# A linear-attention and top-1 MoE kernel: a hand-ordered pipeline over the batches, the expert blocks in two tables, w1 in two halves, unordered scatters

## The chip, the cores and the metric

The kernel runs on one core of one Trainium2 chip. The metric is the device time of one execution in microseconds (us), and of several executions the median. TensorE is called PE, VectorE DVE, ScalarE ACT, GpSimd POOL and SyncE SP. POOL and SP also hand transfers to DMA queues.

## The reference

Two steps follow each other. The first is linear attention over 8 batches with 8 heads, 576 positions and 64 channels, with relu and a cosine and a sine weight of the position. The second is a top-1 mixture of experts on the 4608 rows of 512 numbers that come out.

```
k_p = concat(relu(k) * cos, relu(k) * sin);  q_p likewise
kv  = einsum('bhsf,bhsd->bhfd', k_p, v);  z = k_p.sum(s)
num = einsum('bhsf,bhfd->bhsd', q_p, kv); den = einsum('bhsf,bhf->bhs', q_p, z) + 1e-6
x = (num / den), rows of 512
logits = x @ w_gate;  expert = argmax;  gate = softmax(logits)[expert]
h = relu(x @ w1[expert]);  out = gate * (h @ w2[expert])   # 8 experts, 512 -> 1024 -> 512
```

An expert takes at most 1152 rows; rows above that give zero.

## The kernel before

**Attention, one batch after the other.** A batch loads k, v and q (1.18 MB each, fp32) over SP's queue: k and v in rows of 1 KB (L173), q in transfers that gather 256-byte pieces (L168). ACT takes the relu of k (L185). DVE multiplies v with the cosine and the sine table in 16 operations of 128x256 and 4 tails of 64x256 (L196, L200). PE makes the kv products (L211), transposes them (L217) and makes the gate columns from them (L223), so that the attention product gives the router's logits too. PE transposes q (L234), and ACT takes the relu while it moves q out of PSUM (L235). Ten units follow: PE forms p (L252) in one of two PSUM buffers, ACT scales half of it (L258), DVE adds the other half and writes `num` (L260).

**Router.** A chain of small DVE operations (L266 to L328) divides, finds each row's expert and, with a few small PE products (L296 to L309) and the running count `carry`, the row's slot. DVE and POOL write the scaled rows in bf16 with the token's number behind them (`xg`, L336), and POOL scatters them in five indirect transfers into the DRAM buffer `xd` (L341), which keeps a region for each expert. Behind each batch's scatters POOL issues one expert's w1 (L347, 2.1 MB read as fp32, 1 MB written as bf16).

**Experts.** After the last batch POOL issues eight pieces of w2 (L353), ACT writes zero rows behind each expert's last row (L360), and DVE makes one table of 43 blocks (L363 to L402): a block is 128 rows of one expert, and the table holds its expert and its first row. `first(i)` fetches a block transposed (`xT`, L420) and its token numbers (`ids`, L422), multiplies with w1 (`h_ps`, L431, 8 matmuls), relu on ACT (L434), and transposes on PE (L437) into `hT` (L439). `second(i)`, 17 blocks behind, multiplies with w2 (`y_ps`, L448), copies on ACT or DVE in turn into one of four `y` buffers (L452, L454) and scatters the rows to `out` (L455).

**What sets the order.** The tile framework's scheduler places each engine's instructions from the program as written, and adds the waits. Both kinds of scatter are declared free of dependences within a group (L344, L458), but no instruction is a member of that group, so that each scatter waits for the landing of the one before; this is seen in the waits below.

Of the kernel before, what the change touches and what calls it, by code (L numbers as in the profile page):

```python
# [26 lines left out]
def kernel(  # L27
# [99 lines left out]
    carry = state.tile([P, E], FP32, name="carry", tag="carry")  # L127
    nc.vector.tensor_copy(out=carry[:], in_=base[:])

    scatters = "xd rows"  # L130

    with ExitStack() as p1:
        pc = p1.enter_context(tc.tile_pool(name="pc", bufs=1))

        vs_t = []
        for i in range(2):
            t_ = pc.tile([P, NC, HB, 2, D + 1], FP32, name=f"vs{i}")
            for c in range(NC):
# [12 lines left out]
        kvp = p1.enter_context(tc.tile_pool(name="kvp", bufs=2))
        kv1 = p1.enter_context(tc.tile_pool(name="kv1", bufs=1))
# [5 lines left out]
        def load(src, b, name):  # L158
# [17 lines left out]
            if name != "q":  # L176
                nc.sync.dma_start(out=t[:], in_=src[b, :, NJ * P:S, :].rearrange("h p d -> p h d"))
# [228 lines left out]
    with ExitStack() as p2:  # L406
# [93 lines left out]
```

## Time and profile of the kernel before

| what | value |
|---|---|
| three executions | 550.68 us median (548.35 to 555.81) |
| profiled execution | 557.07 us, span of its instructions 555.3 us |
| mean granted clock of PE | 0.836 of full speed |
| busy: PE, DVE, ACT, POOL | 357.1, 213.6, 159.3, 133.5 us |
| moved by DMA | 66.98 MB, mean 121 GB/s |
| from the start to batch 1's kv products | 45.35 us |
| batches 1 to 7 | 45.35 to 257.90 us |
| w2 awaited | 257.90 to 317.60 us |
| experts | 317.60 to 555.30 us |

The shares of busy time are means over stages that differ, so the stretches are read apart. The granted clock is a share of full speed: 1.0 is 2.4 GHz and 0.5 is 1.2 GHz. "A <- B" in a list of waits says that A stood idle until B was done. In the chain that ended last, each piece is what released the next; "issue" is time in which nothing that the profile shows was awaited.

### The profile page before, as it was taken

Reading aid. Unit: us, or ns where it says so; the run is one execution under the profiler, and the core shown is the slowest. Engines: PE = TensorE matmul, PEld = TensorE weight load, DVE = VectorE, ACT = ScalarE, POOL = GpSimd, SP = SyncE. Lnnn points to the kernel's source line nnn. Section 1 sums busy time; section 2 is a strip of 40 time slices with the busy share of each in tenths; the row PEclk is TensorE's granted clock in tenths of the full one; section 3 lists DMA queues with packets and bytes.
Section 4 is the critical chain, followed back from the end, with each engine's and each line's share of the span. In section 5 each row is a group of like instructions: output and inputs, shape, how many; then the busy total and the mean of one; then the engine's idle time right before and its main releaser. Section 6 shows DMA issues by size and latency. Waiting matters only on the chain.

```text
span 555.3 us, 8309 instructions
## 1 busy us (share of the span) xinstructions
PE 357.1 (64%) x2672; PEld 222.3 (40%) x2672; DVE 213.6 (38%) x614; ACT 159.3 (29%) x288; POOL 133.5 (24%) x159
## 2 busy tenths in 40 slices
PE   0867675695886767671000187999999988895520
PEld 0645555573764646461000043444444433442210
DVE  1468582665839386738200013222222222210000
ACT  4262604225251525241000042433333323310000
POOL 4003251232423233434340000002222212222222
PEclk9897867669767779797555598999999999999985
DMA  5983879688776753518999931424334231011210
GB/s 152 235 208 105 213 132 263 120 210 173 184 173 124 194 86 111 87 39 156 163 186 223 178 52 30 77 48 86 86 85 111 61 86 57 29 73 54 77 67 30
DMA packets 113449, 66.98 MB, mean 121 GB/s; under 512 B 80151, under 2 KB 105751, under 8 KB 113408
## 3 DMA queue, kind: packets, MB, share of 16 engines
q0 software_dynamic: 17776, 31.37, 26.9%
q1 hardware_dynamic: 94480, 34.02, 26.8%
q10 hardware_dynamic: 1152, 1.05, 0.7%
q8 instruction: 24, 0.39, 0.3%
q14 instruction: 17, 0.14, 0.1%
HBM read 61.92 MB, written 17.06 MB: 142 GB/s over the span
## 4 chain that ended last, share of the span: by engine, by line
PE 38%; DMA 29%; issue 11%; DVE 10%; ACT 7%; SPq 3%; POOL 1%; POOLq 0%; DVEq 0%; ACTq 0%
DMA out_dram<-y,idx 15%; PE kv_ps L211 10%; PE h_ps L431 9%; PE p_ps L252 6%; DMA w_sb<-in_moe_w_dram 5%; PE y_ps L448 5%; DMA km<-in_k_dram 4%; DVE num L260 4%; ACT tmp L258 3%; DMA xd<-xg,slot_i 3%; PE ht_ps L437 2%; PE q_ps L234 2%; PE g_ps L223 1%; ACT km L185 1%; DVE lg L272 1%
## 5 line engine op out<-in xcount | busy, mean ns | idle before, releaser
L431 PE MATMUL h_ps<-w_sb,xT 128*128 x344 | 87.3, 390 | 61.7 <-DMA w_sb<-in_moe_w_dram 60.0
L448 PE MATMUL y_ps<-w_sb,hT 128*128 x344 | 82.5, 378 | 20.6 <-DVE y L454 8.1
L455 POOL DMA_INDIRECT out_dram<-y,idx x43 | 41.8, 972 | 217.1 <-ACT h L434 96.1
L434 ACT ACTIVATE h<-h_ps 128x512 bf16<-128x512 f32 x86 | 51.4, 597 | 143.5 <-PE h_ps L431 143.5
L252 PE MATMUL p_ps<-kva,rq 64*128 64x146 f32 (+1 forms) x640 | 64.9, 338 | 21.4 <-DVE num L260 20.0
L341 POOL DMA_INDIRECT xd<-xg,slot_i x40 | 46.6, 1165 | 123.1 <-DMA xd<-xg,slot_i 75.4
L431 PEld LDWEIGHTS <-xT 128*128 128x128 bf16 x344 | 33.6, 100 | 97.7 <-DMA xT<-xd 58.9
L260 DVE SCALAR_TENSOR_TENSOR num<-p_ps,sintab,tmp 128x292 f32<-128x292 f32 (+1 forms) x80 | 40.9, 519 | 67.1 <-ACT tmp L258 63.4
L252 PEld LDWEIGHTS p_ps<-kva,rq 64*128 64x128 f32 (+1 forms) x640 | 50.7, 206 | 33.4 <-DVE num L260 30.3
L211 PE MATMUL kv_ps<-vs,km 128*64 128x130 f32 x512 | 51.8, 365 | 14.5 <-DVE vs L196 14.5
L448 PEld LDWEIGHTS <-hT 128*128 128x128 bf16 x344 | 32.8, 97 | 56.3 <-issue 26.3
L439 DVE COPY hT<-ht_ps 128x1024 bf16<-128x1024 bf16 x43 | 29.6, 690 | 55.6 <-PE ht_ps L437 52.0
L424 DVE TENSOR_TENSOR idx<-ids,pen 128x1 int32<-128x1 int32 x43 | 6.8, 159 | 114.6 <-DMA ids<-xd 72.0
L258 ACT ACTIVATE tmp<-p_ps,costab 128x292 f32<-128x292 f32 (+1 forms) x80 | 39.9, 503 | 33.4 <-PE p_ps L252 29.2
L211 PEld LDWEIGHTS kv_ps<-vs,km 128*64 128x64 f32 x512 | 40.8, 187 | 21.7 <-issue 21.6
L437 PE MATMUL ht_ps<-identb,h 128*128 128x128 bf16 x344 | 34.4, 223 | 9.6 <-DVE hT L439 5.1
L336 POOL TENSOR_TENSOR xg<-num,rden 128x512 bf16<-128x512 f32 x16 | 23.1, 1464 | 67.0 <-DVE rden L328 58.8
L437 PEld LDWEIGHTS <-h 128*128 128x128 bf16 x344 | 22.8, 99 | 36.0 <-ACT h L434 27.1
L454 DVE COPY y<-y_ps 128x512 f32<-128x512 f32 x22 | 15.2, 692 | 52.0 <-DMA out_dram<-y,idx 37.4
L452 ACT COPY y<-y_ps 128x512 f32<-128x512 f32 x21 | 12.3, 587 | 71.8 <-DMA out_dram<-y,idx 36.2
L336 DVE TENSOR_TENSOR xg<-num,rden 128x512 bf16<-128x512 f32 (+1 forms) x24 | 27.1, 1182 | 0.2
L196 DVE TENSOR_SCALAR vs<-vm,costab 128x256 f32<-128x256 f32 x64 | 22.3, 348 | 11.0 <-DMA vm<-in_v_dram 10.8
(113 smaller groups left out, 296.1 us busy)
## 6 DMA issues: line engine op xcount, KB each, us to landing
w_sb<-in_moe_w_dram POOLq DMA_DIRECT2D x16, 1024.0 KB, 10.1
km<-in_k_dram SPq DMA_DIRECT2D x16, 512.0 KB
vm<-in_v_dram SPq DMA_DIRECT2D x16, 512.0 KB
qm<-in_q_dram SPq DMA_DIRECT2D x64, 128.0 KB
xd<-zrow ACTq DMA_DIRECT2D x8, 128.5 KB
kt<-in_k_dram SPq DMA_DIRECT2D x8, 128.0 KB
vt<-in_v_dram SPq DMA_DIRECT2D x8, 128.0 KB
qt<-in_q_dram SPq DMA_DIRECT2D x32, 32.0 KB
```

The source lines that it names most:

```text
L211: nc.tensor.matmul(out=kv_v[o * D:(o + 1) * D, r, :, :], lhsT=lhsT, rhs=rhs, start=(c == 0), stop=(c == NC - 1))
L252: nc.tensor.matmul(out=p_ps[0:rows, o, r, 0:2 * KW], lhsT=rq[o * D:(o + 1) * D, 2 * u + r, c * P:c * P + rows], rhs=kva[o * D:(o + 1) * D, ...
L258: nc.scalar.activation(out=tmp[0:rows], in_=p_v[0:rows, :, 0:KW], func=ACT.Copy, scale=costab[0:rows, c:c + 1])
L260: nc.vector.scalar_tensor_tensor(out=num[0:rows, c, u * HB:(u + 1) * HB, :], in0=p_v[0:rows, :, KW:2 * KW], scalar=sintab[0:rows, c:c + 1] ...
L336: eng.tensor_tensor(out=xg[0:rows, c, 0:DT].rearrange("p (h d) -> p h d", h=H), in0=num[0:rows, c, :, 0:D], in1=rden[0:rows, c, :].unsquee ...
L341: si = nc.gpsimd.indirect_dma_start(out=xd[:, :], out_offset=bass.IndirectOffsetOnAxis(ap=slot_i[0:rows, c:c + 1], axis=0), in_=xg[0:rows, ...
L431: nc.tensor.matmul(out=h_ps[:], lhsT=xT[:, g, :], rhs=w1_sb[:, bass.ds(e1, 1), g, n * 512:(n + 1) * 512], start=(g == 0), stop=(g == G - 1))
L434: nc.scalar.activation(out=h[:, n * 512:(n + 1) * 512], in_=h_ps[:], func=ACT.Relu)
L437: nc.tensor.transpose(out=t_ps[:, f, :], in_=h[:, f * P:(f + 1) * P], identity=identb[:])
L439: nc.vector.tensor_copy(out=hT[:], in_=t_ps[:])
L448: nc.tensor.matmul(out=y_ps[:], lhsT=hT[:, f, :], rhs=w2_sb[:, bass.ds(e2, 1), f, :], start=(f == 0), stop=(f == FB - 1))
L455: oi = nc.gpsimd.indirect_dma_start(out=out[:, :], out_offset=bass.IndirectOffsetOnAxis(ap=idx[:, 0:1], axis=0), in_=y[:], in_offset=None, ...
```

## The change

All instructions are now placed by the program's own order (`tc.manual_schedule()`). `run()` merges several lists of steps by a fraction between 0 and 1 that each list gets. An iteration `it` of the attention holds three stages: `stage_a(it)` (relu of k, scaling of v, q's transposes, kv products and gate columns), `stage_p(it-1)` (the ten p units) and `stage_r(it-2)` (router and scatters). Loads are issued an iteration ahead. q comes in rows of 1 KB, and its relu goes to POOL (`relu_q`, four operations of 128x512 and two of 64x256 for a batch). v is scaled in eight operations of 128x512 on DVE, its two tails go to ACT, and so do the two copies of the gate columns. `vs` and `qm` have one buffer.

w1 is held in two halves: `w1a`, columns 0 to 511 of each expert, is loaded in iterations 2 to 8; `w1b` takes memory that the attention frees, so that it comes after it. `table_a` is made after seven batches and holds 24 full blocks; `table_b`, after the last batch's router, holds the other 19. The first halves of seven blocks are multiplied with `w1a` among the steps of the last batch's router. Then w1b's eight pieces, w2's eight pieces, the second halves of the seven blocks, and the loop over the rest, with `down(i)` 17 blocks behind as before. Scatters are now members of their groups. `y` has two buffers in place of four, `xT` ten in place of six.

```diff
-    NB = (N + E * (P - 1)) // P
-    LAG = 17
...
+    NA = -(-(N - S - E * (P - 1)) // P)
+    NB = (N + E * (P - 1)) // P - NA
+    HA, HX = 7, 18
+    LAG = 17
+    FIRST = 7
...
+    def free_of(ins, group):
+        tc.declare_no_dep(ins.ins, group=group, reason=DISJOINT)
+
+    def member(ins, group):
+        tc.add_to_no_dep_group(group, ins.ins)
+
+    def run(*streams):
+        order = []
+        for n, (steps, lo, hi) in enumerate(streams):
+            for i, f in enumerate(steps):
+                order.append((lo + (hi - lo) * (i + 0.5) / len(steps), n, i, f))
+        for _, _, _, f in sorted(order, key=lambda t: t[:3]):
+            f()
+
+    ctx.enter_context(tc.manual_schedule())
...
+    yp = ctx.enter_context(tc.tile_pool(name="yp", bufs=2))
...
+        for name, src in (("k", k), ("v", v), ("q", q)):
+            pl = io1 if name == "q" else io
+            m = pl.tile([P, H, NJ, D], FP32, name=name + "m", tag=name + "m")
+            t = pl.tile([D, H, D], FP32, name=name + "t", tag=name + "t")
+            nc.sync.dma_start(out=m[:], in_=src[b, :, 0:NJ * P, :].rearrange("h (p j) d -> p h j d", j=NJ))
+            nc.sync.dma_start(out=t[:], in_=src[b, :, NJ * P:S, :].rearrange("h p d -> p h d"))
+            loaded[b][name] = (m, t)
...
-                            nc.sync.dma_start(out=m[:, r, :, o, :],
-                                              in_=sv[r, 0:NJ * P, o, :].rearrange("(p j) d -> p j d", j=NJ))
...
+        def relu_q(w):
+            def f():
+                u, r = w // 2, w % 2
+                nc.gpsimd.tensor_scalar(
+                    out=qr[:, w, :, :, :].rearrange("p j o d -> p o j d"),
+                    in0=qm[:, u * HB + r:u * HB + r + 3:2, :, :], scalar1=0.0, scalar2=None, op0=ALU.max)
...
+                if c == NJ:
+                    nc.scalar.activation(out=vs[0:rows, c, :, t, 0:D], in_=src, func=ACT.Copy,
+                                         scale=tab[0:rows, c:c + 1])
...
+        steps += [emit(0), emit(1), emit(2), scatter(0), emit(3), scatter(2), emit(4), scatter(1), scatter(4),
+                  scatter(3)]
...
+                free_of(si, "xd rows")
+                if b == B - 1:
+                    free_of(si, "early reads")
+                member(si, "xd rows")
...
+    def w1_piece(n, e):
+        def f():
+            nc.gpsimd.dma_start(out=w1h[n][:, e, :, :],
+                                in_=moe_w1[e].rearrange("(g p) f -> p g f", p=P)[:, :, n * 512:(n + 1) * 512])
...
+    load(0)
+    for it in range(B + 1):
+        streams = []
+        if it < B:
+            load(it + 1)
+            elem, rls, qs, kvst = stage_a(it)
+            streams += [(elem, 0.0, 0.5), (rls, 0.0, 0.3), (qs, 0.1, 0.5), (kvst, 0.45, 1.0)]
+        if 1 <= it:
+            streams.append((stage_p(it - 1), 0.05, 0.97))
+        if 2 <= it:
+            streams.append((stage_r(it - 2, ps_a, "a"), 0.0, 1.0))
+            streams.append(([w1_piece(0, it - 2)] + ([w1_piece(0, 7)] if it == B else []), 0.9, 1.0))
+        run(*streams)
+    table_a()
...
+        ti = nc.sync.dma_start(out=xT[:], in_=xd[bass.ds(r0, P), 0:DT], transpose=True)
+        ids = const.tile([P, 2], BF16, name=f"ids{i}")
+        di = nc.sync.dma_start(out=ids[:], in_=xd[bass.ds(r0, P), DT:XW])
+        if i < NA:
+            member(ti, "early reads")
+            member(di, "early reads")
...
+    def up(i, n):
...
+        h = hp.tile([P, F // 2], BF16, name="h", tag=f"h{n}")
...
+            nc.tensor.matmul(out=h_ps[:], lhsT=bl["xT"][:, g, :], rhs=w1h[n][:, bass.ds(e1, 1), g, :],
...
+        y = yp.tile([P, DT], FP32, name="y", tag="y")
...
+        free_of(oi, "out rows")
+        member(oi, "out rows")
...
+    htx = []
+    firsts = [lambda i=i: fetch(i) for i in range(2)]
+    for i in range(FIRST):
+        firsts.append(lambda i=i: fetch(i + 2))
+        firsts.append(lambda i=i: up(i, 0))
+        if i >= 1:
+            firsts.append(lambda i=i: turn(i - 1, 0))
+    firsts.append(lambda: turn(FIRST - 1, 0))
+    run((firsts, 0.0, 1.0), (stage_r(B - 1, ps_y, "y"), 0.0, 0.6), ([table_b], 0.6, 0.7),
+        ([w1_piece(1, e) for e in range(E)], 0.65, 1.0))
     for e in range(E):
         nc.gpsimd.dma_start(out=w2_sb[:, e, :, :], in_=moe_w2[e].rearrange("(g p) d -> p g d", p=P))
...
-        yp = p2.enter_context(tc.tile_pool(name="yp", bufs=4))
...
-            tc.declare_no_dep(oi.ins, group="out rows", reason=DISJOINT)
...
-        for i in range(NB + LAG):
-            if i < NB:
-                first(i)
-            if i >= LAG:
-                second(i - LAG)
+    nump.release()
+    rt.release()
+    htx.append(ctx.enter_context(tc.tile_pool(name="htx", bufs=HX)))
+    NBLK = NA + NB
+    for i in range(FIRST):
+        up(i, 1)
+        if i >= 1:
+            turn(i - 1, 1)
+    turn(FIRST - 1, 1)
+    for i in range(FIRST, NBLK + LAG):
+        if FIRST + 2 <= i + 2 < NBLK:
+            fetch(i + 2)
+        if i < NBLK:
+            up(i, 0)
+            up(i, 1)
+        if FIRST <= i - 1 < NBLK:
+            turn(i - 1, 0)
+            turn(i - 1, 1)
+        if 0 <= i - LAG:
+            down(i - LAG)
```

**PE in one batch of the attention.** Before, PE's row of a batch from the second half of the kv products on (`kv_ps`, `t_ps` and `g_ps` its transposes and gate columns, `q_ps` and `qt_ps` q's transposes, `p_ps` the p units):

```order
L211 MATMUL kv_ps<-vs_151,km 64x130 x8
L211 MATMUL kv_ps<-vs_151,kt 64x130 x2
L217 MATMUL t_ps<-ident,kvt 128x128 x4
L223 MATMUL g_ps<-wg_sb,t_sb 128x32 x4
L234 MATMUL q_ps<-ident,qm 128x128 x16
L240 MATMUL qt_ps<-ident,qt 128x64 x4
L252 MATMUL p_ps<-kva,rq 128x146 x32
L252 MATMUL p_ps<-kva,rq 64x146 x8
```

After, the end of one iteration and the start of the next on PE (`p_ps` belongs to the batch before that of `kv_ps` and `q_ps`):

```order
L291 MATMUL kv_ps<-vs,km 64x130 x8
L291 MATMUL kv_ps<-vs,kt 64x130 x2
L329 MATMUL p_ps<-kva,rq 64x146 x4
L303 MATMUL t_ps<-ident,kvt 128x128 x4
L329 MATMUL p_ps<-kva,rq 64x146 x4
L312 MATMUL g_ps<-wg_sb,t_sb 128x32 x4
L329 MATMUL p_ps<-kva,rq 128x146 x4
L262 MATMUL q_ps<-ident,qr 128x128 x4
L329 MATMUL p_ps<-kva,rq 128x146 x4
```

The p units no longer stand in one piece behind their own batch's transposes, but one at a time among another batch's kv products and transposes.

**POOL at the last batch and the weights.** Before (`xd` the scatters of the last batch, `w_sb` w2; DMASW is a lane of POOL's transfers, and a wait on it is for a landing):

```order
L341 DMA xd<-xg,slot_i 37888x514 [waits DMASW3_49]
L353 DMA w_sb<-in_moe_w_dram 128x8x512
L341 DMA xd<-xg,slot_i 37888x514 [waits DMASW5_49]
L353 DMA w_sb<-in_moe_w_dram 128x8x512
L341 DMA xd<-xg,slot_i 37888x514 [waits DMASW7_49,DMASW1_49]
```

After, the same place, with the last scatters of the last batch and the first pieces of `w1b`:

```order
L493 DMA xd<-xg,slot_i 37888x514 [waits DMASW6_49,DVE_49]
L493 DMA xd<-xg,slot_i 37888x514 [waits DMASW7_49,Pool_49]
L508 DMA w1b<-in_moe_w_dram 128x4x512 [waits DMAHW3_49,DMAHW2_49,DMAHW4_49,DMASW0_49,DMAHW5_49,PE_49,Activation_49]
L508 DMA w1b<-in_moe_w_dram 128x4x512 [waits DMASW1_49]
L508 DMA w1b<-in_moe_w_dram 128x4x512 [waits DMASW2_49]
```

The weights stood between the scatters; now all of `w1b`, and behind it all of w2, stand behind the last scatter, and the first piece waits for the attention's readers.

**POOL at the end.** Before, the scatters to `out`, each with the lane of the scatter ahead of it:

```order
L455 DMA out_dram<-y,idx 4608x512 [waits DMASW5_49,DMASW4_49,Activation_49]
L455 DMA out_dram<-y,idx 4608x512 [waits DMASW6_49,DMASW5_49,DVE_49]
L455 DMA out_dram<-y,idx 4608x512 [waits DMASW7_49,DMASW6_49,Activation_49]
L455 DMA out_dram<-y,idx 4608x512 [waits DMASW7_49,DVE_49]
L455 DMA out_dram<-y,idx 4608x512 [waits DMASW0_49,Activation_49]
```

After:

```order
L693 DMA out_dram<-y,ix 4608x512 [waits DMASW0_49,DVE_49]
L693 DMA out_dram<-y,ix 4608x512 [waits DMASW1_49,DVE_49,Activation_49]
L693 DMA out_dram<-y,ix 4608x512 [waits DMASW2_49,DVE_49]
L693 DMA out_dram<-y,ix 4608x512 [waits DMASW3_49,DVE_49,Activation_49]
L693 DMA out_dram<-y,ix 4608x512 [waits DMASW4_49,DVE_49]
```

Each now waits for its own lane alone, which is that of the scatter eight before it, and for its `y`.

## Rows read from the trace of the kernel before

**Rows 1.** Stretches: length, busy time (count) of PE, PEld, DVE, ACT, POOL; clock, DMA share, GB/s.

```profile
45.35:257.90 212.55, 151.00 (x1436) 120.63 (x1435) 133.87 (x392) 76.40 (x150) 70.31 (x63) 0.79 0.66 150
257.90:317.60 59.70, 0.01 (x1) 0.11 (x2) 8.57 (x29) 0.00 (x0) 15.68 (x15) 0.50 1.13 189
317.60:369.30 51.70, 44.90 (x275) 22.01 (x275) 13.38 (x35) 20.31 (x34) 0.00 (x0) 0.93 0.34 53
431.00:489.00 58.00, 49.98 (x281) 23.00 (x280) 14.04 (x29) 16.78 (x29) 11.63 (x12) 1.00 0.21 59
489.00:555.30 66.30, 30.03 (x133) 12.65 (x131) 6.23 (x9) 4.69 (x8) 17.44 (x18) 0.86 0.16 60
```

**Rows 2.** The same columns for single batches, from kv products to kv products.

```profile
73.65:108.73 35.08, 24.24 (x207) 19.68 (x209) 19.22 (x58) 11.23 (x22) 11.22 (x11) 0.69 0.75 173
202.93:230.47 27.54, 19.26 (x207) 15.48 (x209) 19.70 (x58) 9.69 (x20) 9.89 (x9) 0.87 0.43 94
```

**Rows 3.** Waits of POOL: us in all, times, longest.

```profile
POOL xd L341 <- DMA xd<-xg,slot_i: 75.4, 19, 7.5
POOL out_dram L455 <- DMA out_dram<-y,idx: 49.6, 18, 5.3
```

**Rows 4.** The chain that ended last, 264 to 318 us: start, length, what.

```profile
264.26 0.94 POOL w_sb L353
...
290.36 27.19 DMA w_sb<-in_moe_w_dram
317.59 3.57 PE h_ps L431 x8
```

**Rows 5.** Timeline of PE, one batch: start, length, engine, line, operation, count, idle before.

```profile
202.86 2.00 PE L211 MATMUL kv_ps<-vs,km 128*64 128x130 f32 x16
...
210.01 1.11 PE L211 MATMUL kv_ps<-vs,km 128*64 128x130 f32 x16
...
211.41 0.98 PE L217 MATMUL t_ps<-ident,kvt 128*128 128x128 f32 x4
213.39 1.08 PE L223 MATMUL g_ps<-wg_sb,t_sb 128*128 128x32 f32 x8 [0.99 <-ACT t_sb L219]
214.30 1.95 PE L234 MATMUL q_ps<-ident,qm 128*128 128x128 f32 x16
...
218.42 1.27 PE L252 MATMUL p_ps<-kva,rq 64*128 64x146 f32 x16 [0.73 <-DVE num L260]
```

**Rows 6.** The chain that ended last, in the p units of an earlier batch.

```profile
158.24 2.50 PE p_ps L252 x16
```

**Rows 7.** Groups by form, DVE, 45 to 258 us: operation, count, busy, mean ns, idle before.

```profile
L260 DVE SCALAR_TENSOR_TENSOR num<-p_ps,sintab,tmp 128x292 f32<-128x292 f32 x56 | 28.6, 521 | 52.9 <-ACT tmp L258 49.2 <-ACT rq L242 2.5 <-issue 1.1
L196 DVE TENSOR_SCALAR vs<-vm,sintab 128x256 f32<-128x256 f32 x48 | 17.1, 357 | 0.0
L200 DVE TENSOR_SCALAR vs<-vt,sintab 64x256 f32<-64x256 f32 x12 | 4.2, 348 | 0.1
```

**Rows 8.** Groups by form, POOL, the whole span.

```profile
L341 POOL DMA_INDIRECT xd<-xg,slot_i x40 | 46.6, 1165 | 123.1 <-DMA xd<-xg,slot_i 75.4 <-issue 18.8 <-DVE num L260 17.5
...
L336 POOL TENSOR_TENSOR xg<-num,rden 128x512 bf16<-128x512 f32 x16 | 23.1, 1464 | 67.0 <-DVE rden L328 58.8 <-DVE last L373 8.1
```

**Rows 9.** The chain that ended last in the steady part of the experts, one block to the next.

```profile
373.46 1.73 PE h_ps L431 x8
...
377.68 1.80 PE h_ps L431 x8
```

**Rows 10.** Timeline at the end: an evict, its scatter and w2's matmuls, and the last scatter.

```profile
516.49 0.69 DVE L454 COPY y<-y_ps 128x512 f32<-128x512 f32 x1 [6.29 <-DMA out_dram<-y,idx]
517.14 0.97 POOL L455 DMA_INDIRECT out_dram<-y,idx  x1 [2.51 <-DMA out_dram<-y,idx]
517.24 1.89 PE L448 MATMUL y_ps<-w_sb,hT 128*128 x8 [1.72 <-DVE y L454]
...
549.17 0.97 POOL L455 DMA_INDIRECT out_dram<-y,idx  x1 [2.41 <-DMA out_dram<-y,idx]
```

More of the change, by code (lines that the diff above doesn't have):

```diff
@@ new lines @@
+    tmpp = pool("tmpp", 2)
+    ps_a = pool("ps_a", 4, bass.MemoryType.PSUM)
+    ps_p = pool("ps_p", 2, bass.MemoryType.PSUM)
+    vs = io1.tile([P, NC, H, 2, D + 1], FP32, name="vs")
+    for c in range(NC):
+        for t, tab in ((0, costab), (1, sintab)):
+            nc.gpsimd.tensor_copy(out=vs[:, c, :, t, D:D + 1],
+                                  in_=tab[:, c:c + 1].unsqueeze(1).to_broadcast([P, H, 1]))
+    num_t = []
+    for i in range(2):
+        t_ = nump.tile([P, NC, H, KW], FP32, name=f"num{i}")
+        nc.gpsimd.memset(t_[D:P, NJ, :, :], 1.0)
+        num_t.append(t_)
@@ L314 @@
[L314 to L317 removed]
+            nc.tensor.matmul(out=st["d"][:, 0, :], lhsT=ub[0:D, :], rhs=oh[0:D, NJ, :], start=False, stop=False)
+            nc.tensor.matmul(out=st["d"][:, 1, :], lhsT=onesb[0:D, :], rhs=oh[0:D, NJ, :], start=False, stop=True)
@@ L338, with scatter, f @@
                     in1=rden[0:rows, c, :].unsqueeze(2).to_broadcast([rows, H, D]), op=ALU.mult)
-            for c in range(NC):
+            return f
+        def scatter(c):
+            def f():
                 rows = P if c < NJ else D
@@ new lines, in table_b @@
+    def table_b():
+        end_i = tp.tile([P, E], I32, name="end_i")
+        nc.vector.tensor_copy(out=end_i[:], in_=carry[0][:])
+        for e in range(E):
+            r0 = nc.values_load(end_i[0:1, e:e + 1], engines=[ACTE], min_val=e * REG, max_val=e * REG + N,
+                                skip_runtime_bounds_check_because=INRANGE)
+            zi = nc.scalar.dma_start(out=xd[bass.ds(r0, P), :], in_=zrow[:])
+            free_of(zi, "xd rows")
+            free_of(zi, "early reads")
+            member(zi, "xd rows")
+        todo = whole("b", True)
+        nc.vector.tensor_tensor(out=todo[:], in0=todo[:], in1=tabs["done"][:], op=ALU.subtract)
+        tbl, _, pn = table("b", NB, todo[:], tabs["done"], True)
+        tabs["b"], tabs["pen"] = tbl, pn
@@ new lines, in up @@
+    def up(i, n):
+        bl = blocks[i]
+        tbl, m = where(i)
+        e1 = nc.values_load(tbl[0:1, 0, m:m + 1], engines=[PE], min_val=0, max_val=E - 1,
+                            skip_runtime_bounds_check_because=INRANGE)
+        h = hp.tile([P, F // 2], BF16, name="h", tag=f"h{n}")
+        h_ps = ps_h.tile([P, 512], FP32, name="h_ps", tag="h")
+        for g in range(G):
+            nc.tensor.matmul(out=h_ps[:], lhsT=bl["xT"][:, g, :], rhs=w1h[n][:, bass.ds(e1, 1), g, :],
+                             start=(g == 0), stop=(g == G - 1))
+        nc.scalar.activation(out=h[:], in_=h_ps[:], func=ACT.Relu)
+        bl["h", n] = h
```

590 lines of the change are left out of this document (332 added, 258 removed).

## The prediction

> **What bounds the kernel now.** I read the stretches first, then the single batches, the waits, the chain that ended last, and last the timelines. Batches 1 to 7 take 212.55 us, 30.4 us each. No engine fills them: PE is busy for 151.00 us, DVE for 133.87, and the DMA share is 0.66 [rows 1]. A batch's own steps stand in a row, so the engines wait for each other: DVE's `num` additions alone were preceded by 49.2 us of waiting for ACT's `tmp` [rows 7]. PE also runs slowly. The granted clock is 0.79 in this stretch, 0.69 in the slowest batch (35.08 us) and 0.87 in a fast one (27.54 us) [rows 1, 2]; sixteen p matmuls take 2.50 us at the low level (1.2 GHz) and 1.27 at the high one (2.4 GHz) [rows 5, 6]. Then come 59.70 us with PE at rest, in which w2 is awaited: its first piece is issued at 264.26 and the first expert matmuls start at 317.59 [rows 1, 4]. The experts follow. While up and down run together a block takes 377.68 − 373.46 = 4.2 us, nearly all PE [rows 9]. From 431 us on PE is the bound no more: scatters wait for scatters, 49.6 us in 18 waits [rows 3], and in the last 66.30 us PE is busy for 30.03 [rows 1].
>
> **The attention.** All of PE's work in an iteration at the high level: kv four times 211.41 − 210.01, 5.6; t 0.98; g 1.08; q's transposes and tail 2.4; five pairs of p units at 1.27, 6.35; the router's products 0.7: 17.1 us [rows 5]. (The last two small numbers are read from the row of q, 1.95, and its tail, and from the gaps of the same batch.) DVE is busy 19.70 us in a batch now [rows 2]. It loses sixteen operations of 0.357 and four of 0.348 (7.1 us) and two small copies (0.4, an estimate), and gains eight operations of 128x512. No row of DVE has that form: below lies 0.357 for half the size, above twice that, 0.71 [rows 7]. I take 0.61, nearer to the upper end because it is twice the work: 4.9. DVE's sum is 17.1. ACT gets v's tails and the gate copies and gives nothing back in number of operations (q's still move out of PSUM on ACT): about 13 from the 9.69 to 11.23 of now [rows 2], no bound. POOL gets the relu of q. The row for a 128x512 operation on POOL is 1.464, with two inputs; below it I only have DVE's 0.357 for half the size. I take 1.0 for each of four and 0.6 for each of two, 5.2 us; with two `xg` (2.9), five scatters (5.8 by their mean of 1.165) and one weight issue (0.94) POOL has 15 us [rows 4, 8]. The scatters no longer wait for each other: 75.4 us of POOL's idle time goes [rows 3], but POOL was not the bound in the attention, and I count nothing for it. It is covered by the two engines at 17.
>
> An iteration isn't as short as its busiest engine, since `vs` has one buffer. In its first half DVE must scale v (4.9), half of the p units (5 times 0.521) and half of the router chain (about 3.2), so 11 us, before the kv products can run; in the second half PE has kv, half of p and the gate columns, 10.6, and the evictions between them, about 2.5 [rows 5, 7]. That gives **24 us an iteration**, against 30.4. The bounds: 20, if the halves overlap so that DVE's 17.1 and some 3 us of waits are left; 31, if PE stays at the low level, where 2.00 stands for 1.11 [rows 5]: 17.1 by 1.8. Iteration 0 waits for all of q before the transposes and has no other batch to work on; I take 40 us (before, batch 1's kv products begin at 45.35, [rows 1], with the router of batch 0 already in it). Iteration 1 lacks the router: 20. Six full ones 144, and iteration 8, without `stage_a`, 14: the last `num` at 218, the table 3.3 behind it, so T0 = 221. Before, that stretch ends at 257.90. **Gain in the attention: 36 us.** q in rows of 1 KB instead of 256 bytes takes load off SP's queue; the DMA share is 0.66 on average, so the loads are hidden by the 24 us of an iteration (and if they weren't, 3.54 MB at the 173 GB/s of a busy batch take 20 us, less than 24) [rows 1, 2].
>
> **The weights.** Half of w1 is now late: w1b (8.4 MB read) is loaded after the attention, with w2 (16.8 MB) behind it in the same queue. What waits: POOL's first w1b issue stands behind the last batch's scatters, and those behind its router, whose PE products stand behind the first `up` of block 0, which waits for batch 6's scatters and the last pieces of w1a. I take 9 us for that, 9 more for the router chain, 3 for `xg` and 5 for the five scatters: first issue at T0 + 26 (20 to 35). The rate: w2's 16.8 MB took 317.59 − 264.26 = 53.3 us, with the DMA share at 1.13 [rows 1, 4]. The 25.2 MB take 80 us by that, and with the blocks' fetches among them I take 91. So the last w2 piece lands at W2 = T0 + 117 = 338, later than the 317.6 of now. This eats most of what the attention gave. By the Trainium skill, page "DMA: Bandwidth & Descriptors", section "Specifications", a core's share of the memory is about 358 GB/s, so that 25.2 MB would take 70 us and the sum would be 10 us lower; the trace's own rate is 315 GB/s, and it is the one that I use.
>
> **The experts.** In the time to W2 PE does up of 17 blocks in two helpings, with pauses of some 26 and 19 us. The downs wait for all of w2. From W2: 1.73 for the first down, 25 pairs at 4.25 [rows 9], 106.3; then 17 downs alone. Now each costs the serial scatter: the evict to `y`, 0.1, the landing, next scatter, 3.4 us a block (66.30 us for the last of them) [rows 1, 10]. Unordered, a block costs the larger of PE's matmuls (1.89 for eight, [rows 10]), POOL's 0.97, and half of a turn of `y`'s two buffers, which is the evict, 0.69, and the landing. From one scatter's start to the next pass 0.97 + 2.51, and the next evict lies in that, so a landing comes about 2.8 after its start [rows 10]: (0.69 + 0.1 + 2.8)/2 = 1.8. I take 1.8, 30.6 us. PE starts after pauses at the low level: 6 us lost, as the clock of 0.93 over 51.70 us cost about 4 now [rows 1]. The last scatter's end: 6.8, from 555.3 − 549.17 = 6.1 and its evict [rows 10]. W2 + 1.7 + 106.3 + 30.6 + 6 + 6.8 = W2 + 151.4 = 489.5 us of span. Now the same part, from 317.59 to 555.3, is 237.7 us, of which 17 ups (about 44 us) move ahead of W2 and the rest is the scatters'.
>
> **Sum.** 489.5 against a span of 555.3; the profiled execution adds 1.8 (557.07), so 491.3. That execution stands 6.4 us above the median of 550.68, and I take it off: **485 us**.
>
> **Rivals.**
> - *The halves overlap and the clock stays high.* Two batches' products in one stream leave PE fewer gaps. T = 20 and no loss by the clock: 6 × 4 + 6 less, about 455 us. For it: DVE's 17.1. Against it: the single `vs`.
> - *PE stays at the low level through the attention.* T = 31, the attention gains nothing: 6 × 7 more, 42 us, and the early up blocks slow as well (about 12): some 540, no change. For it: PE would be busy for 17 of 24 us, a smaller load than the 24.24 of 35.08 us that stands beside clock 0.69 [rows 2]. By the Trainium skill, page "TensorE: Matmul & The Clock Gate", section "HAM oscillation — how this bites in real kernels", idle gaps between groups of matmuls drop the clock again and again; the trace agrees in that the first eight up matmuls after the 59.70 us at rest took 3.57 us, later ones 1.73.
> - *Two `y` buffers bring the tail back.* If a landing takes 6 us with several scatters under way, in place of 2.8, a block costs 3.4 us in the tail: 17 × 1.6 more, about 512 us. For it: POOL's longest wait for a landing was 5.3 us [rows 3]. Against it: it was one of 18 that came to 49.6.
> - *POOL's queue decides, and the kernel gets slower.* The relu of q stands in POOL's order ahead of `xg` and the scatters of another batch, and q's transposes wait for it. If one operation on its strided form takes 4 us instead of 1.0, POOL's sum is 27 and its chain, in which `relu_q` waits for q and `xg` for the router, about 36: 6 × 12 more, then the later w1a and scatters, 571 us. It decides from T = 33 on. Against it: 1.464 for the two-input operation of that size [rows 8].
>
> **How the numbers follow.** Main case 0.55 (its own range 470 to 510: T from 22 to 26, 12 us each way, and 8 us of the weights' 91); the fast attention 0.19; y's buffers 0.10; the low clock 0.10; POOL 0.06. The range 455 to 530 takes in the first three, 0.84, and leaves out no change and slower. About 2% (11 us) can be told from no change: faster 0.84, within 2% 0.10, slower 0.06.
>
> **What would show it.** Right: iterations of 24 us from one batch's kv products to the next; DVE operations on `vs` of 0.6 and `qr` on POOL of 1.0; the first w1b issue near 247 us and the last w2 landing near 338; pairs of 4.25 with no wait for w2 after that; the last 17 downs at 1.8, with no scatter waiting for a scatter. Wrong: clock under 0.7 in the attention; `qr` above 2 us; evicts that wait for scatters in the list of waits; w1b and w2 taking over 100 us, which would put each microsecond on the end.

## The result and the profile after

| | before | after |
|---|---|---|
| median, lowest and highest of four executions | 553.24 us (548.35 to 556.31) | 501.01 us (497.33 to 501.60) |
| profiled execution, its span | 557.07, 555.3 us | 497.33, 495.5 us |
| ratio of the times | | 0.905 (95%: 0.896 to 0.914) |
| mean granted clock of PE | 0.836 | 0.852 |
| busy: PE, DVE, ACT, POOL | 357.1, 213.6, 159.3, 133.5 us | 349.4, 185.3, 170.6, 192.1 us |

The change is faster by 9.5%. Forecast were 485 us and faster; 501 lies in the range of 455 to 530. The steps behind that number came out worse and better than forecast, by amounts that mostly cancel, so they are read one by one. Two profiled executions below are slow ones, those of the run with ordered scatters to `xd` (574.85 us, median 562.3) and of the run with w1b in iteration 8 (498.69 us, median 492.8).

The stretches of the changed kernel, in the columns of [rows 1]: one iteration of the attention, the first 31 us of awaiting weights, the rest of that time, the blocks in which up and down run together, and the end.

```profile
143.21:170.67 27.46, 19.66 (x206) 15.06 (x206) 14.98 (x45) 12.96 (x27) 16.63 (x16) 0.81 0.60 170
275.12:306.37 31.25, 2.90 (x13) 1.48 (x13) 2.23 (x8) 1.20 (x2) 13.02 (x17) 0.50 1.17 190
306.37:356.50 50.13, 37.17 (x225) 19.16 (x224) 10.53 (x27) 17.32 (x29) 0.07 (x1) 0.87 1.28 192
356.50:457.62 101.12, 101.12 (x616) 51.91 (x616) 28.16 (x66) 37.10 (x63) 24.42 (x25) 0.99 0.35 92
457.62:495.50 37.88, 30.48 (x139) 13.19 (x136) 8.88 (x28) 5.07 (x9) 17.50 (x18) 0.96 0.20 77
```

Against [rows 1, 2]: this iteration takes 27.5 us in place of the 27.5 to 35.1 of a batch, at a clock of 0.81 in place of 0.69 to 0.87. From one batch's kv products to the next's, which is called the pitch below, five iterations take 142.5 us (73.88 to 216.41), 28.5 each. The blocks in which up and down run together fill PE wholly (101.12 of 101.12 us), at 3.9 us a block in place of the 4.2 of [rows 9]. The end takes 37.9 us in place of 66.3. The time in which weights are awaited has become longer, 81.4 us from 275.12 to 356.50 in place of 53.3 [rows 4], but PE is busy for 40 of them. The span is 59.8 us shorter: w2 is first used 38.9 us later than the experts began before (356.5 against 317.6), and what follows takes 98.7 us less (139.0 against 237.7), in part because 17 ups now stand ahead of it.

**What closes an iteration.** The timeline of PE in the same iteration (columns as in [rows 5]), then a wait:

```profile
169.29 1.08 PE L312 MATMUL g_ps<-wg_sb,t_sb 128*128 128x32 f32 x8
170.67 1.00 PE L329 MATMUL p_ps<-kva,rq 64*128 64x146 f32 x8 [0.30 <-ACT kva L315]
177.28 1.12 PE L262 MATMUL q_ps<-ident,qr 128*128 128x128 f32 x4 [5.62 <-POOL qr L217]
```

```profile
PE q_ps L262 <- POOL qr L217: 28.1, 5, 5.7
```

That is PE's wait for `qr` from 60 to 230 us (us in all, times, longest). POOL, and DVE in the next iteration:

```profile
165.32 1.55 POOL L485 TENSOR_TENSOR xg<-num,rden 128x512 bf16<-128x512 f32 x1 [9.41 <-DVE rden L478]
167.04 1.10 POOL L493 DMA_INDIRECT xd<-xg,slot_i  x1 [0.17 <-POOL xg L485]
...
174.32 1.03 POOL L493 DMA_INDIRECT xd<-xg,slot_i  x1 [0.30 <-issue]
175.42 0.24 POOL L374 TENSOR_SCALAR xg<-tok_i 128x5 int32<-128x5 int32 x1
175.74 5.84 POOL L217 TENSOR_SCALAR qr<-qm 128x512 f32<-128x512 f32 x4
...
193.67 1.55 POOL L485 TENSOR_TENSOR xg<-num,rden 128x512 bf16<-128x512 f32 x1 [10.30 <-DVE rden L478]
```

```profile
180.32 0.52 DVE L336 SCALAR_TENSOR_TENSOR num<-p_ps,sintab,tmp 128x292 f32<-128x292 f32 x1 [5.14 <-ACT tmp L334]
...
183.68 0.19 DVE L411 TENSOR_TENSOR oh<-key,kmx 128x40 bf16<-128x40 f32 x1
...
193.39 0.19 DVE L478 TENSOR_TENSOR rden<-rden,gate 128x40 f32<-128x40 f32 x1
```

PE has done the gate columns and one p unit by 171.7 and then waits 5.6 us for `qr`. POOL makes `qr` at 175.74, not because q is late, but because `xg` and five scatters stand ahead of it in POOL's order. These wait for `rden`, the end of another batch's router, whose small operations stand in DVE's order between `num` additions that wait, over ACT's `tmp`, for PE: the one at 180.32 waits 5.14 us, as PE had waited for `qr`. So the loop is: `qr`, PE's products, DVE's router, `xg`, scatters, the next `qr`. POOL is busy for 16.6 of 27.5 us and idles for nearly 11 of them, and yet its order sets the pitch; the first experiment below tests this. The sizes of the operations with new forms, by groups:

```profile
L217 POOL TENSOR_SCALAR qr<-qm 128x512 f32<-128x512 f32 x32 | 46.8, 1485 | 30.5 <-DMA qm<-in_q_dram 30.1
L245 DVE TENSOR_SCALAR vs<-vm,costab 128x512 f32<-128x512 f32 x32 | 16.6, 518 | 15.1 <-DMA vm<-in_v_dram 15.1
L245 DVE TENSOR_SCALAR vs<-vm,sintab 128x512 f32<-128x512 f32 x32 | 15.6, 487 | 0.0
```

**Where the weights' time begins.** PE's timeline around the last batch's router, POOL's issues, and PE at the first w2 products:

```profile
259.68 1.87 PE L660 MATMUL h_ps<-w1a,xT 128*128 x4 [18.07 <-DMA xT<-xd]
261.35 0.31 PE L424 MATMUL c_ps<-oh,ub 128*128 128x32 bf16 x4
```

```profile
275.12 6.08 POOL L508 DMA_DIRECT2D w1b<-in_moe_w_dram  x8
...
305.56 0.87 POOL L711 DMA_DIRECT2D w_sb<-in_moe_w_dram  x1 [2.27 <-DMA w1b<-in_moe_w_dram]
```

```profile
356.50 3.34 PE L681 MATMUL y_ps<-w_sb,hT 128*128 x8 [6.48 <-DMA w_sb<-in_moe_w_dram]
```

In PE's order the router's products (`c_ps`) stand behind the first block's `up`, which waits 18 us for its rows. They lead to the last scatters, and these to w1b's first issue at 275.12. From there the 25.2 MB that w1b and w2 read take until 356.5.

### The profile page after: what moved, and what is told of

It is laid out like the page before. It is cut to its first block, busy times and chain, and to the rows that moved or that the text cites. A ratio compares the mean times of both kernels' runs of the same rounds, so it can differ in the third digit from the quotient of the medians.

```text
span 495.5 us, 8167 instructions
## 1 busy us (share of the span) xinstructions
PE 349.4 (71%) x2672; PEld 219.3 (44%) x2672; DVE 185.3 (37%) x544; ACT 170.6 (34%) x319; POOL 192.1 (39%) x205
## 4 chain that ended last, share of the span: by engine, by line
PE 31%; issue 24%; POOL 19%; DMA 15%; SPq 4%; DVE 3%; ACT 2%; another core or an unknown queue 1%; POOLq 1%; ACTq 0%; DVEq 0%
PE h_ps L660 13%; PE y_ps L681 9%; POOL qr L217 7%; POOL xd L493 5%; DMA xT<-xd 5%; DMA out_dram<-y,ix 4%; DMA qm<-in_q_dram 4%; PE ht_ps L671 3%; PE kv_ps L291 2%; POOL xg L485 2%; PE p_ps L329 2%; DMA ids<-xd 2%; POOL qrt L222 2%; POOL out_dram L693 1%
## 5 line engine op out<-in xcount | busy, mean ns | idle before, releaser
L329 PE MATMUL p_ps<-kva,rq 64*128 64x146 f32 (+1 forms) x640 | 77.0, 356 | 3.9 <-ACT kva L315 2.4
L672 DVE COPY hT<-ht_ps 128x512 bf16<-128x512 bf16 x86 | 33.2, 420 | 119.8 <-PE ht_ps L671 107.9
L660 PE MATMUL h_ps<-w1a,xT 128*128 x172 | 47.2, 399 | 43.1 <-DMA xT<-xd 43.0
L693 POOL DMA_INDIRECT out_dram<-y,ids x24 | 23.4, 977 | 121.6 <-DVE y L687 84.0
L262 PE MATMUL q_ps<-ident,qr 128*128 128x128 f32 x128 | 30.0, 377 | 53.3 <-POOL qr L217 53.3
L217 POOL TENSOR_SCALAR qr<-qm 128x512 f32<-128x512 f32 x32 | 46.8, 1485 | 30.5 <-DMA qm<-in_q_dram 30.1
L660 PE MATMUL h_ps<-w1b,xT 128*128 x172 | 47.3, 401 | 15.0 <-DMA ids<-xd 14.9
L262 PEld LDWEIGHTS q_ps<-ident,qr 128*128 128x128 f32 x128 | 19.3, 188 | 60.8 <-POOL qr L217 56.6
L291 PE MATMUL kv_ps<-vs,km 128*64 128x130 f32 x512 | 39.9, 303 | 0.0
L264 ACT COPY rq<-q_ps 128x512 f32<-128x512 f32 x32 | 18.6, 581 | 45.8 <-PE q_ps L262 45.7
```

The costliest lines, as they stand in the source:

```text
L217: nc.gpsimd.tensor_scalar(out=qr[:, w, :, :, :].rearrange("p j o d -> p o j d"), in0=qm[:, u * HB + r:u * HB + r + 3:2, :, :], scalar1=0.0 ...
L262: nc.tensor.transpose(out=q_ps[:, j, :], in_=qr[:, w, j, :, :].rearrange("p o d -> p (o d)"), identity=ident[:])
L291: nc.tensor.matmul(out=kv_v[o * D:(o + 1) * D, w % 2, :, :], lhsT=lhsT, rhs=rhs, start=(c == 0), stop=(c == NC - 1))
L329: nc.tensor.matmul(out=p_ps[0:rows, o, r, 0:2 * KW], lhsT=rq[o * D:(o + 1) * D, 2 * u + r, c * P:c * P + rows], rhs=kva[o * D:(o + 1) * D, ...
L660: nc.tensor.matmul(out=h_ps[:], lhsT=bl["xT"][:, g, :], rhs=w1h[n][:, bass.ds(e1, 1), g, :], start=(g == 0), stop=(g == G - 1))
L672: nc.vector.tensor_copy(out=bl["hT"][:, n * (FB // 2):(n + 1) * (FB // 2), :], in_=t_ps[:])
```

## The experiments

Each is the changed kernel (501 us) with one edit, unless it says otherwise. Times are medians of four executions (of five with ordered scatters to `xd`); the kernel before ran beside them and had medians of 553.5 to 556.3 us.

### The relu of q ahead of the scatters in POOL's order

```diff
...
-            streams += [(elem, 0.0, 0.5), (rls, 0.0, 0.3), (qs, 0.1, 0.5), (kvst, 0.45, 1.0)]
...
+            streams += [(elem, 0.0, 0.5), (qs, 0.1, 0.5), (kvst, 0.45, 1.0)]
+            if it + 1 < B:
+                streams.append(([relu_q(it + 1, w) for w in range(4)], 0.52, 0.66))
```

> Edit: the relu of q of the next batch is placed on POOL at 0.52 to 0.66 of an iteration, ahead of the other batch's xg and scatters, in place of the start of its own iteration, behind them. Theory A (POOL's order closes the iteration: q's relu stands behind five scatters that end the iteration before it): PE's waits for qr, 28.1 us between 60 and 230 us, go, the kv products of successive batches come 23 us apart instead of 28.5, and the time falls by 25 to 30 us from 501, to about 473. Rival B (PE's own work at the lower clock, or DVE, sets 28.5 us, and POOL is only late because they are): the pitch stays above 27 us and the time within 5 us of 501.

480.6 us, 20 less; ratio to before 0.866 (0.860 to 0.872). Two iterations of it, in the columns of [rows 1], then PE's wait for the router's `oh` from 60 to 220 us, in the changed kernel and in this run:

```profile
98.76:122.84 24.08, 20.08 (x207) 15.62 (x206) 15.28 (x44) 12.80 (x26) 16.38 (x15) 0.85 0.67 190
122.84:146.84 24.00, 20.01 (x206) 15.61 (x205) 14.98 (x44) 12.81 (x26) 15.65 (x15) 0.86 0.69 193
```

```profile
PE c_ps L424 <- DVE oh L411: 11.0, 6, 3.9
PE c_ps L428 <- DVE oh L415: 25.1, 7, 4.1
```

The same operations with the same lengths (`qr` 1.490 us) stand in another place, and the pitch falls from 28.5 us to 24.7 on the mean of five (73.00 to 196.41), 24.0 in the middle three. PE's wait for `qr` is gone from the list. Theory A holds in kind; the fall of the pitch (to 23) and the gain (25 to 30) were expected somewhat larger. POOL's relu does not hold the 24.0, since the next run has no relu on POOL and nearly the same pitch. PE's largest wait is now that for `oh`, in the router's chain on DVE; whether it sets the pitch was not tested.

### q loaded and its relu taken as before

```diff
+                for w in range(4):
+                    for o in range(2):
+                        nc.sync.dma_start(out=m[:, w, :, o, :],
+                                          in_=src[b, head(w, o), 0:NJ * P, :].rearrange("(p j) d -> p j d", j=NJ))
...
-                nc.scalar.copy(out=rq[:, w, 0:NJ * P].rearrange("p (j s) -> p j s", j=NJ), in_=q_ps[:])
+                nc.scalar.activation(out=rq[:, w, 0:NJ * P].rearrange("p (j s) -> p j s", j=NJ), in_=q_ps[:], func=ACT.Relu)
```

> Edit: q is loaded in 256-byte pieces, eight transfers and four tails for a batch, straight into the order in which PE transposes it, and ACT takes the relu while it evicts, as in the kernel before; nothing of q is on POOL. Theory A: the same gain as with the relu put ahead, 25 to 30 us, to about 473, since loads are hidden by an iteration of 23 us. Rival C (the short pieces load the queue of SP so much that q is late): PE waits for q in most iterations, the DMA share rises to 0.75 or more, and the time is 490 or above.

474.1 us, 27 less; 0.856 (0.850 to 0.861).

```profile
120.27:144.09 23.82, 19.82 (x207) 15.51 (x206) 14.67 (x44) 12.84 (x26) 9.01 (x9) 0.86 0.74 197
```

The pitch is 23.8 us, POOL's busy time 9.0 in place of 16.6, and ACT's is the 12.8 of the run before: the relu in the eviction costs nothing that the copy did not. The DMA share rises to 0.74, near the 0.75 of rival C, but from 60 us on PE waits for no load. At the start PE's first transposes come at 20.5 us in place of the 23.6 of the run before, since q does not pass POOL first. So these two parts of the change, the relu on POOL and the 1 KB rows that call for it, cost 27 us together.

### q in 256-byte pieces alone

```diff
+            if name == "q":
+                for j in range(NJ):
+                    nc.sync.dma_start(out=m[:, :, j, :], in_=sv[:, :, j, :])
```

> Edit: q's main part comes in four transfers of 256-byte pieces for a batch in place of one of 1 KB rows; its relu stays on POOL as in the changed kernel. Theory K (loads are hidden by iterations of 28 us, so the row length matters only at the start): the first qr begins 1 to 5 us later, the pitch stays at 28.5, and the time rises by 1 to 6 us. Rival C (the longer rows were a part of the gain): the pitch rises above 30 and the time by 12 us or more.

503.7 us against 501.0; 0.908 (0.898 to 0.918), where the changed kernel has 0.905 (0.896 to 0.914). The kv products of successive batches come 27.5 to 29.2 us apart, and the first `qr` starts at 23.93 in place of 22.61. Theory K holds: the longer rows are worth nothing that could be told from none, so that by these two runs it is the relu on POOL that costs the 27 us.

### Scatters to xd in order

```diff
-                member(si, "xd rows")
```

> Edit: the scatters to xd are no longer members of their group, so that each of a batch's five waits for the landing of the one before, as in the kernel before; all else is the changed kernel. Theory A (POOL's order closes the iteration, so all that stands between rden and the next batch's qr counts): four waits of 2.5 to 4 us a batch more, the pitch of the kv products goes from 28.5 to about 40 us, and the time rises by 60 to 85 us, above the kernel before. Rival B (POOL has slack): under 15 us.

562.3 us, 61 more, and some 1.5% above the kernel before: 1.015 (1.009 to 1.022). An iteration, PE's wait for `qr` in it, and the waits of the whole run (us in all, times, longest):

```profile
118.65:159.53 40.88, 22.07 (x207) 16.90 (x206) 14.93 (x44) 13.06 (x26) 16.46 (x15) 0.71 0.42 114
```

```profile
148.48 1.12 PE L262 MATMUL q_ps<-ident,qr 128*128 128x128 f32 x4 [16.68 <-POOL qr L217]
```

```profile
PE q_ps L262 <- POOL qr L217: 105.1, 9, 24.2
...
POOL xd L493 <- DMA xd<-xg,slot_i: 45.8, 20, 4.1
```

The pitch is 40 to 42 us. In this iteration POOL waits 4.97, 3.64, 2.31 and 1.38 us before the four later scatters, 12.3 in all (the list puts the first down to DVE, the others to landings), and PE waits 16.7 us for `qr` in place of 5.6: POOL's waits reach PE nearly in full. In the kernel before POOL waited for longer, 75.4 us [rows 3]. By the orders shown that should have cost PE little, since nothing of the next batch stood behind it; no run takes the order away there. The unordered scatters and the relu on POOL belong together: with the second, the first are worth 61 us.

### Scatters to out in order

```diff
-        member(oi, "out rows")
```

> Edit: the scatters to out are no longer members of their group, so that each waits again for the landing of the one before. Theory F (order costs only where a block takes less than a landing): the pairs of up and down keep 3.9 us, the 17 downs at the end go from 1.9 to 3.4 us each, plus 26 us, to about 527. Rival G (the chain of landings binds in the pairs too, as from 431 us on in the kernel before, 5 us a block): plus 26 and 25 times 0.6 to 1.1, 40 to 55 us. Rival H (two y buffers already make the evicts wait): under 5 us.

527.2 us, 26 more; 0.953 (0.947 to 0.958). The pairs of up and down, then the end:

```profile
361.11:463.12 102.01, 101.38 (x605) 52.12 (x617) 28.08 (x66) 37.12 (x63) 24.42 (x25) 0.98 0.33 92
463.12:524.90 61.78, 32.85 (x136) 13.47 (x136) 8.83 (x28) 5.06 (x9) 17.49 (x18) 0.93 0.12 48
```

The pairs keep their time (102.0 against 101.1 us), and the end takes 61.8 us in place of 37.9, 23.9 more, near the 66.3 of before the change. Theory F holds. That the median comes out at its 527 to the microsecond is in part luck: in the profiled executions 4.6 us more lie ahead of the pairs (361.11 against 356.50), where the edit changes nothing.

### Four y buffers

```diff
-    HA, HX = 7, 18
+    HA, HX = 7, 17
...
-        y = yp.tile([P, DT], FP32, name="y", tag="y")
+        y = (ypx[0] if i // 2 % 2 else yp).tile([P, DT], FP32, name="y", tag="y")
```

> Edit: four y buffers in place of two (for their room nine xT buffers in place of ten, and 17 of the later hT in place of 18). Theory I (with unordered scatters two buffers hold the last 17 downs at 1.9 us against PE's 1.73): the waits of the evicts for landings, 44.6 us in all, go, and the time falls by 2 to 3 us. Rival (the buffers cost the kernel most of what unordered scatters gave): 10 us or more. Rival (the other two sizes were tight): slower by over 3 us.

493.5 us; 0.891 (0.883 to 0.899), an interval that overlaps that of the changed kernel. The changed kernel's last downs, then this run's:

```profile
457.62 10.52 PE L681 MATMUL y_ps<-w_sb,hT 128*128 x48
468.45 3.61 PE L681 MATMUL y_ps<-w_sb,hT 128*128 x16 [0.31 <-DVE y L687]
...
488.52 1.89 PE L681 MATMUL y_ps<-w_sb,hT 128*128 x8 [0.22 <-DVE y L687]
```

```profile
455.38 29.52 PE L681 MATMUL y_ps<-w_sb,hT 128*128 x133
```

The last downs run without a gap, 29.5 us in place of 32.8. This is the 3 us of theory I; the rest of the 7.5 us between the medians is not explained by the buffers.

### The last batch's router ahead of the first blocks

```diff
...
-    run((firsts, 0.0, 1.0), (stage_r(B - 1, ps_y, "y"), 0.0, 0.6), ([table_b], 0.6, 0.7),
-        ([w1_piece(1, e) for e in range(E)], 0.65, 1.0))
+    run((stage_r(B - 1, ps_y, "y"), 0.0, 0.6), ([table_b], 0.6, 0.7),
+        ([w1_piece(1, e) for e in range(E)], 0.65, 0.9), (firsts, 0.9, 1.0))
```

> Edit: after the attention the whole router of the last batch stands ahead of the first halves of the seven blocks on PE, DVE and ACT, where now the first up waits 18 us for its block and the router's products stand behind it; the nine fetches are issued first. Theory D (the weights' chain sets the end: the first w1b issue waits for the last scatters, and all of w2 for w1b): the first w1b issue moves from 275.1 to about 261, the first w2 matmul from 356.5 to about 343, and the time falls by 13 us, to about 488. Rival E (the end is set by PE's blocks, and early blocks that are now done later take back what the weights gain): less than 4 us.

497.1 us, 3.9 less, with no interval to tell that from none. The router's products, the issues, and the first w2 products:

```profile
256.54 0.29 PE L424 MATMUL c_ps<-oh,ub 128*128 128x32 bf16 x4 [10.46 <-DVE oh L411]
...
268.01 6.07 POOL L508 DMA_DIRECT2D w1b<-in_moe_w_dram  x8
...
353.17 3.57 PE L681 MATMUL y_ps<-w_sb,hT 128*128 x8 [8.86 <-DMA w_sb<-in_moe_w_dram]
```

The issue came 7 us earlier, not 14: the router then waited 10.46 us for `oh`, its own chain on DVE, which had been hidden behind the first block. And the weights took 85.2 us in place of 81.4. Theory D's number was not reached. The gain lies just under the 4 us of rival E, but not for its reason: PE still waits 8.86 us for `w_sb`, so the weights still come last.

### One early half block in place of seven

```diff
-    FIRST = 7
+    FIRST = 1
...
-    NX = FIRST + 3
+    NX = 10
```

> Edit: one block in place of seven has its first half multiplied ahead of w1b, with the number of xT buffers kept. Theory L (the early half blocks are work that PE could as well do in the time in which it awaits w2, where it still idles for 6.5 us): six halves of 1.3 us move into that time, 8 us, and the time changes by less than 3 us. Rival M (early blocks are a part of the gain): slower by 8 us or more.

489.2 us, 12 less; 0.880 (0.873 to 0.887). With fewer steps ahead, the order of the merged lists also puts the router's products (257.32) ahead of the first `up`, as in the run above, and w1b's first issue comes at 268.79. Beside that run:

```profile
350.59 1.02 PE L660 MATMUL h_ps<-w1b,xT 128*128 x4
352.05 1.89 PE L681 MATMUL y_ps<-w_sb,hT 128*128 x8
```

PE comes to the first w2 product with no wait for w2 and at the high clock (1.89 us against 3.57), since more was left for it to do; the six moved halves cost nothing. So six of the seven early half blocks gain nothing here: in the changed kernel PE idles 6.5 us before w2 in any case. Theory L holds in kind, but not in its number (under 3 us): that the kernel became faster was not expected. The order of the router is a part of it, and this run doesn't tell it from the rest.

### w1b in iteration 8

```diff
+        if it == B:
+            io1.release()
+            io.release()
...
+            else:
+                streams.append(([w1_piece(1, e) for e in range(E)], 0.0, 0.1))
```

> Edit: the buffers of k, v, q and vs are released after the last batch's kv products, and w1b is loaded there during iteration 8, ahead of batch 6's scatters, in place of after the last batch's scatters; the last three pieces of w1a come in iteration 7. w2 stands where it stood. Theory D (the chain last scatter, w1b, w2 sets the end): w1b's first issue comes at about 228 us, w2's first landings begin at 275, the first w2 matmul moves from 356.5 to about 330, and the time falls by 25 to 28 us, to about 474. Rival E (PE then has too much left to do before w2, or w1b's load delays batch 6's scatters and the first blocks): under 12 us.

492.8 us, 8 less; 0.886 (0.878 to 0.894). A scatter of batch 6, w2's issues, and on PE the first block and the first w2 product; then the relu of the last batch's q, in the changed kernel and in this run:

```profile
259.90 1.08 POOL L493 DMA_INDIRECT xd<-xg,slot_i  x1 [1.47 <-DMA w1b<-in_moe_w_dram]
...
292.59 7.17 POOL L717 DMA_DIRECT2D w_sb<-in_moe_w_dram  x8
```

```profile
277.12 1.87 PE L667 MATMUL h_ps<-w1a,xT 128*128 x4 [26.05 <-DMA xT<-xd]
...
355.54 1.89 PE L688 MATMUL y_ps<-w_sb,hT 128*128 x8
```

```profile
204.08 5.84 POOL L217 TENSOR_SCALAR qr<-qm 128x512 f32<-128x512 f32 x4
...
211.93 5.84 POOL L217 TENSOR_SCALAR qr<-qm 128x512 f32<-128x512 f32 x4
```

Rival E holds, in its second form. This execution is 7.9 us behind the changed kernel's before the edit can matter (211.93 against 204.08), and this is to be taken off what follows. Batch 6's scatters now stand behind w1b's issues and wait for landings of it (1.47 and 1.62 us), and the first block's fetch stands behind them: the first `up` comes at 277.1 in place of 259.7, some 9.5 us of it by the edit. The router stands behind it, and w2's first issue comes at 292.6 in place of 283.5, some 1 us later by the edit. So the 27 us that w1b no longer takes (an estimate, 8.4 MB at 310 GB/s) are lost ahead of w2's issue. From there to the first w2 product pass 63 us in place of 73, and PE no longer waits for w2 at its end.

### Three edits together

The first run has q as before the change, w1b in iteration 8, and the router first; the second adds that the second table and the zero rows stand behind the first blocks; the third is the first with one early half and four y buffers.

> Edit: three together: q loaded and its relu taken as in the kernel before, w1b loaded in iteration 8, and the last batch's router ahead of the first blocks. If the three gains are on one path and add: 27 and 26 and 4 to 8 us, about 442 us. If PE becomes the bound between the attention and w2 (17 ups and their fetches in about 55 us): 455 or more.

> Edit: as with the three edits together (label best, 457 us), but the second table and the zero rows stand behind the first halves of the seven blocks, not ahead, since ACT's relu of these blocks waited 17 us behind the issues of the zero rows. If PE is the bound from the first block on: the waits of 17 us go, the first w2 matmul comes 10 to 17 us earlier unless w2 has not landed (its last piece is issued at about 248 and needs about 55 us), and the time falls by 5 to 10 us, to about 449. If w2 then takes over as the last to come: under 4 us.

> Edit: the three edits of label best, with one early half block in place of seven (and so one early hT buffer in place of seven) and four y buffers in place of two. If early halves and two y buffers only cost, as their own runs suggest: 3 us from the tail and up to 5 from the time before the first w2 matmul, about 449 us against 457. If with w1b early the seven halves do real work ahead of the first w2 matmul: 457 or more.

457.0 us, 0.826 (0.821 to 0.832); 460.8 us, 0.833 (0.828 to 0.838); 457.1 us, 0.821 (0.818 to 0.825). All three beat both kernels. The first gains 44 us; its three edits alone gained 27, 8 and 4, or 39, so together they are worth about their sum, though the 4 can't be told from none. More was expected, chiefly of w1b in iteration 8. In the first, PE waits no longer for w2 but for ACT and the fetches:

```profile
243.38 1.87 PE L661 MATMUL h_ps<-w1a,xT 128*128 x4 [16.86 <-DMA xT<-xd]
251.90 1.86 PE L661 MATMUL h_ps<-w1a,xT 128*128 x4 [6.65 <-DMA xT<-xd]
270.69 0.61 PE L672 MATMUL ht_ps<-identb,h 128*128 128x128 bf16 x4 [16.92 <-ACT h L663]
```

Moving the zero rows (second) took most of that wait for ACT away (5.7 us of such waits on PE in place of 18.0), but the fetches then came one in 4 us, and the first w2 product moved from 313.6 to 320.8. With one early half (third) the tail gained its 3 us, and the first w2 product came at 317.95, 4.3 us later than in the first: with w1b early, the seven halves seem to save PE time ahead of w2.

## Why the prediction was right, and where it was not

**The main step that failed: "24 us an iteration", and with it the cause given for it.** Measured were 27.7 us (from 61.4 to 227.6 us for six). The prediction took POOL's 15 us as "covered by the two engines at 17", and looked for the bound in the single `vs`. POOL's sum was nearly right (16.6), its place in the chain was not seen: a sum says nothing of an order. The run with the relu moved ahead shows this, at 24.0 to 25.8 us. That this is the forecast's own 24 says nothing for the cause that it gave, the single `vs`, which no run tests. The rival "POOL's queue decides" named the right mechanism with a wrong threshold: it was to decide "from T = 33 on" with operations of 4 us, and it decided at 28 with operations of 1.485 us. With the landings back in the chain (the ordered scatters to `xd`) it came at 40 us and 562 us, near the rival's 571, but by another cost than the rival named.

**Sizes in the attention.** The relu of q on POOL, taken as 1.0 us: 1.485. The scaling of v, taken as 0.61: 0.518 with the cosine and 0.487 with the sine table, 0.9 us less in an iteration. DVE was busy for 15 us and not 17.1, and the rest is chiefly `xg`, which the prediction left as it was: its three operations on DVE take 2.1 us in an iteration, in a batch before they took 3.6. The first two iterations were forecast at 60 us and ended at 61. T0 became about 248 (forecast 221), w1b's first issue 275.1 (247).

**The weights.** 81.4 us from the first issue to the first w2 product, forecast 91; the 80 us by the rate of [rows 4] alone were right, and the 11 us added for the blocks' fetches were too many. By the Trainium skill, page "DMA: Bandwidth & Descriptors", section "Specifications", with about 358 GB/s for a core, it would have been 70 us, an estimate; the trace stays below that rate, with 25.2 MB in 81.4 us, or 310 GB/s. (The 190 and 192 GB/s in the rows fit the bytes written, 12.6 MB of weights in bf16 with the blocks' rows, not the fp32 bytes read.) The first w2 product came at 356.5 instead of 338.

**The experts.** Forecast 151.4 us behind that point, measured 139.0. The pairs take 3.9 us, not 4.25, since `turn` of the block before stands between `up` and `down` and PE's weight loads no longer wait for ACT's `h` within a block: before, 8.0 us in 27 waits from 369 to 431 us, after, none in the list from 362 to 455. 25 times 0.35 is 9 of the 12 us. The last downs took 1.9 us (forecast 1.8), and the loss by the low clock was smaller than 6 us: the stretch shows a clock of 0.99. That unordered scatters to `out` are worth 17 times 1.6, or 27 us, is borne out by the run that puts the order back: 23.9 us more in the end, 26.2 in the median.

**The sum.** +28 us to w1b's issue, −10 for the weights and −12 behind them make +6: a span of 495.5 for 489.5. The median of after lies 4 us above its profiled execution, that of before 4 to 6 below its own, and so 501 stands 16 us above the forecast of 485. Faster, within the range, was right; that the errors cancel is luck.

**Rivals.** The fast attention did not come. The low clock did not either: 0.77 to 0.87 in the six iterations. The reason given for it misread its own numbers, since 17 of 24 us (0.71) is not a smaller load than 24.24 of 35.08 (0.69). The y buffers cost 3 us, not 27: the landings of scatters to `out` stayed near the 2.8 us of [rows 10], 2.9 and 2.6 in the run with the relu ahead (median of each group).

## What to carry to other kernels

In a hand-ordered pipeline, follow one loop through the orders of all engines before the sums of busy time are compared: an operation that the next iteration's first step needs should stand ahead of the steps that end the current one. An engine that idles a third of the time can still set the pitch. And a load or a relu that is moved to a queue that waits for something inherits its waits; take the eviction that is there anyway.

## What was not expected of the hardware

A one-input fp32 operation of 128x512 takes 1.485 us on POOL and 0.487 or 0.518 on DVE. POOL's two-input one that writes `xg` in bf16 takes 1.313 on the mean, 1.55 for the first of a batch and 1.08 for the second: one input was no faster than two here, though the two forms differ in more than that. A scatter on POOL, unordered, follows the one before after about 1.27 us (0.97 and 0.30), where an ordered one to `out` took 3.4. The unordered ones to `xd` land later, though: 6.1 us after their issue in the run with the relu ahead, 3.8 in the kernel before (medians of 40).
